# Three weights among the first loads, stage 0's parts of x between output copies, and attention units every nine products

## The chip, the cores and the metric

One core of one Trainium2 chip runs the whole kernel. The metric is the device time of one execution in microseconds (us), the median of several runs. The profile is of one further execution, taken by the hardware profiler. Engines: PE is TensorE, PEld its weight loads, DVE VectorE, ACT ScalarE, POOL GpSimd, and SP the engine that issues nearly all transfers; each runs its own instructions in program order, and engines wait for one another by semaphores. L522 is line 522 of the kernel.

## The reference

Masked attention for 8 batches of 8 heads (576 tokens, 64 values per head), and a feed-forward layer with the maximum of three products over its 4608 tokens of 512 values:

```python
mask_local = (rel >= 0) & (rel < 32)                    # heads 0 to 3
mask_strided = (rel >= 0) & (pos_q % 32 == pos_k % 32)  # heads 4 to 7
attn = softmax(where(mask, q @ k.T / 8, -1e9))
x = (attn @ v), heads side by side                      # 4608 x 512
h = max(x @ w1, x @ w2, x @ w3)                         # 4608 x 768
out = h @ w_out                                         # 4608 x 512
```

All values are float32. A product in full precision is made of three TensorE products of high and low parts (hi*hi, hi*lo, lo*hi).

## The kernel before, in words

**Attention units.** The attention comes in 32 units: unit n is batch n // 4 and one pair of heads, in the order strided, strided, local, local (`units`, L234). The heads of a pair lie in one quarter of x's 512 columns, so four units complete a batch's tokens. A unit runs through these steps, each named by a letter in the table `OPENING` (L58) and with its number behind it: S scores on TensorE into PSUM `s_ps` (L309, L318, L340); X mask and less the maximum on DVE (L361 to L368); E the exponential on ACT (L384, in one unit L376); N sums, division and transpose on DVE, from `s_ps` to `pt` (L394 to L404); V values on TensorE from `pt` and `v_t` into `o_ps` (L441, L470, L481); H a copy out of `o_ps` on ACT (L495), which is x's high part or x itself; L the low part on DVE (L500). Strided units of batch 1 and later also need U, `paired_queries` (L287): four ACT copies (L295) that lay out the queries in a `pt` tile, ahead of their scores. `pt` has two buffers, and so have queries and keys (`qk_t`) and values (`v_t`).

**Transfers.** SP issues loads and stores in program order, so whatever waits in its queue holds all behind it. First come the loads of the table `LOADS` (L54): `q` loads queries or keys of a unit (two issues), `v` a part of a unit's values (four or five issues), `w` the next of 18 pieces of w1, w2 and w3 (512 KB each). The pieces that `LOADS` leaves over, and six of w_out, follow at its end. Later a unit's loads are issued as an older unit's buffers come free.

**Weights.** Each piece is taken apart exactly into high and low parts: A and K on ACT (L164, L173), L165 on GpSimd, B on DVE (L183, L186), D on GpSimd (L196), C on ACT and GpSimd (L205, L206). A9 and K9, C8 stand for weight 9 and weight 8.

**Tokens 0 to 1023, plainly.** Two chunks of 512 tokens: `ff_in` (F; f and g are its halves, L522) makes one of 18 products x @ w per chunk into one of two PSUM banks, `ff_max` (M, L537 to L543) takes the maximum and splits h, `ff_out` (O, L552) multiplies by w_out, and `ff_store` (Q, L557) copies the result out of the bank on ACT into a `work` tile and has SP store it. Chunk 0 runs in the order of `OPENING`, chunk 1 in the loop at L720, with units 8 to 15 between its products. The half g0 needs x's parts of unit 3, so H3 and L3. T (L230, L231) splits chunk 1's x. `work` tiles are four, shared by the weights' parts, output copies and the sums below.

**Tokens 1024 to 4607, with fewer products.** The 3584 tokens go in four stages of two blocks of 448. Each stage computes two-by-two block products with seven products instead of eight (in the manner of Strassen and Winograd): nine groups (`quad`), each of seven products of six matmuls (L774), so 63 products per stage. The sums of weights that this needs are made by GpSimd during chunk 1 (L585, L593, L609, steps Y and Z and `sums_at`), written to DRAM (`scratch`), and streamed back as tiles `w_stream` (L665), nine tiles deep. The matching sums and parts of x are made by `conversion(s)` (L670): a generator of six parts of ACT casts (L677) and DVE differences (L680, L683), the fourth to sixth of which build on those before; stage 0's parts run among the four last output copies of chunk 1 (L745 to L747, and `list(convert)` for the rest), later stages' parts between a stage's output products. Each product's result is copied out of its bank by ACT (`snap`, L821, or L828), added by GpSimd (L833) and taken into the maximum `h_all` by DVE (L835). The product two behind uses the same bank. At a stage's end `split` (L858, L859) and `out_part` (L868) do h @ w_out, and `store` (L874) copies out.

**Units within the stages.** `before(s, k)` puts units 16 to 31 among the products k of a stage, six in stages 0 and 1 and four in stage 2 (`COUNTS`): `ahead` is S, the load of queries for two units later, and X; `placed` is V, the load of values, H and L. `after` gives E, N and U of the unit ahead two, three and four products later.

Of the kernel before, what the change touches and what calls it, by code (L numbers as in the profile page):

```python
# [40 lines left out]
COUNTS = (6, 6, 4, 0)  # L41
# [3 lines left out]
NJ = DF // P  # L45
# [6 lines left out]


LOADS = """  # L54
q0 q0 w0 w1 w2 w3 q1 q1 w4 q2 q2 v0 w5 v0 v0 v0 q3 q3 w6 v1 v1 v1 w7 w8 v1 v2 v2 v2 v2 v2 v3 v3 v3 v3 v3
q4 q4 v4 v4 v4 v4 w9 w10 w11 w12 w13 q5 q5 v5 v5 v5 v5
"""
OPENING = """  # L58
A0 S0 X0 A1 K0 E0 B0 B1 A2 K1 K2 D0 D1 C0 N0 S1 A3 K3 C1 B2 B3 A4 X1 D2 D3 B4 S2 E1 C2 N1 A5 K4 D4 C3 V0
# [3 lines left out]
B15 F8 W0 W1 W2 A17 X5 D15 M7 K16 C14 B16 F9 E5 C15 M8 K17 D16 B17 F10 W3 W4 N5 M9 M10 D17 F11 W5 A18 A19 B18 C16 K18 S6  # L63
B19 C17 A20 D18 K19 M11 A21 F12 W6 B20 K20 F13 W7 M12 X6 C18 H4 L4 D19 A22 K21 M13 F14 W8 D20 B21 C19 V5 M14 E6
H5 D21 A23 F15 B22 N6 K22 C20 F16 K23 C21 L5 M15 M16 D22 B23 S7 D23 C22 C23 F17 V6 M17 Y0 X7 O0 G7 Q0 T2 T3 O1 O2
N7 H6 U8 L6 Z0 V7 S8 Q1 Y1 T0 H7 X8 Q2 O3 E8 L7 T1 Q3 N8
"""
APART = [int(step[1:]) for step in OPENING.split() if step[0] == "G"]

# [2 lines left out]
def fused_kernel(ctx, tc, qT, kT, qk_loc, qk_str, v_loc, v_str, m_loc, m_str, w1, w2, w3, w_out, out):  # L72
# [214 lines left out]
    def paired_queries(n):  # L287

        t = loaded[n][0]
        qs = att.tile([P, 2, 512], F32, name="pt")  # L290
        to = qs.rearrange("p j (m r q) -> p j r m q", r=2, q=32)
        for x0, q0, w in ((0, 0, NI), (NI, NI, 32 - NI)):
            src = t[:, x0 : x0 + S].rearrange("p (j r m q) -> p j r m q", j=2, r=2, q=NI)
            for j in range(2):
                pin(nc.scalar.copy(out=to[:, j, :, :, q0 : q0 + w], in_=src[:, j, :, :, :w]))  # L295
        loaded[n].append(qs)
# [85 lines left out]
    def exponentials(n):  # L382
        s = state[n][1]
        pin(nc.scalar.activation(out=s, in_=s, func=AF.Exp, scale=SCALE))  # L384

    def probabilities(n):
        s_ps, s, wide, nm, at, axes, sm = state[n]
        if n in APART:
            sums = sm[:, :, :nm]
        else:  # L390
            sm = att.tile([P, 2, MS], F32, name="sm")

            sums = sm[:, :, :nm] if nm * at == 512 else s_ps[:, :, 512 - MS : 512 - MS + nm]
            pin(nc.vector.tensor_reduce(out=sums, in_=s, op=ALU.add, axis=axes))  # L394
        pin(nc.vector.tensor_scalar(out=sums, in0=sums, scalar1=EPS, scalar2=None, op0=ALU.add))
        pin(nc.vector.reciprocal(out=sm[:, :, :nm], in_=sums))
        pin(nc.vector.tensor_tensor(out=s, in0=s, in1=wide(sm), op=ALU.mult))
        state[n] = s_ps, nm, at

    def transposed(n):  # L400

        s_ps, nm, at = state[n]
        pt = att.tile([P, 2, 512], F32, name="pt")
        pin(nc.vector.transpose(pt[:, :, : nm * at], s_ps[:, :, : nm * at]))  # L404
        state[n] = pt
# [107 lines left out]
    def ff_in(c, j, i, heads=(2, 3, 0, 1)):  # L513

        if 2 in heads:
            hs[c, j, i] = bank()
        f_ps = hs[c, j, i]
        hi, lo = x_chunk(c)
        wh, wl = weight[i, j]
        for kc in heads:  # L520
            for n, (w, x) in enumerate(((wh, hi), (wh, lo), (wl, hi))):
                pin(nc.tensor.matmul(  # L522
                    f_ps, w[:, kc, :], x[:, kc, :], start=(kc == 2 and n == 0), stop=(kc == 1 and n == 2)
                ))
# [20 lines left out]
    def ff_out(c, t):  # L545
        f_ps = bank()
        ts = slice(t * P, (t + 1) * P)
        for j in range(NJ):
            hh, hl = hs[c, j]
            wh, wl = weight[None, j]  # L550
            for n, (h, w) in enumerate(((hh, wh), (hh, wl), (hl, wh))):
                pin(nc.tensor.matmul(f_ps, h[:, ts], w, start=(j == 0 and n == 0), stop=(j == NJ - 1 and n == 2)))  # L552
        hs[c, "out", t] = f_ps

    def ff_store(c, t):
        o_sb = wk.tile([P, DO], F32, name="work")
        pin(nc.scalar.copy(out=o_sb, in_=hs.pop((c, "out", t))))  # L557
        pin(nc.sync.dma_start(out=out[c * CH + t * P : c * CH + (t + 1) * P, :], in_=o_sb))
# [77 lines left out]
    for step in OPENING.split():  # L636
        what, n = step[0], int(step[1:])
# [8 lines left out]
    def ahead(n):  # L646

        scores(n)
        list(load_qk(n + 2))
        less_maximum(n)  # L650

    def placed(n):

        values(n)
        list(load_v(n + 2))
        leading(n)
        rest(n)
# [58 lines left out]
    sums_at = {-2: 1, 0: 2, 3: 3, 5: 4, 7: 5, 9: 6, 11: 7, 14: 8}  # L716
    coming, since = None, 0
    convert = iter(())
    paired_queries(9)
    for i in range(3 * NJ + CH // P):  # L720
        if i - 1 in first_bursts and first_bursts[i - 1] < 15:
            placed(first_bursts[i - 1])
        if i in first_bursts:
            if first_bursts[i] < 15:
                coming, since = first_bursts[i] + 1, i
                ahead(coming)
            else:
                placed(15)
        if i < 3 * NJ:
            ff_in(1, i // 3, i % 3)  # L730
        else:
            ff_out(1, i - 3 * NJ)
        if coming and i == since:
            exponentials(coming)
        if coming and i == since + 1:
            probabilities(coming)
            transposed(coming)
            if (coming + 1) % 4 in (0, 1):
                paired_queries(coming + 1)
            coming = None  # L740
        if i < 3 * NJ:
            ff_max(1, i // 3, i % 3)
        else:
            ff_store(1, i - 3 * NJ)
        if i >= 3 * NJ:  # L745
            for _ in range((2, 0, 1, 1)[i - 3 * NJ]):
                next(convert, None)  # L747
            load_next()
            load_next()
        if i - 3 in sums_at:  # L750
            build_high(sums_at[i - 3])
            build_low(sums_at[i - 3])
        if i in sums_at:
            build_sums(sums_at[i])
            build_mix(sums_at[i])
        if i == 3 * NJ - 1:
            late.close()
            plain.close()
            for name, bufs in (("xc", 1), ("wst", AHEAD + 1), ("snap", 8), ("hsp", 3)):
                second[name] = ctx.enter_context(tc.tile_pool(name=name, bufs=bufs, reuse_waits="tile"))  # L760
            convert = conversion(0)
# [6 lines left out]
    def supers():  # L768
# [9 lines left out]

        def before(s, k):

            n = 16 + sum(COUNTS[:s]) + k // 10
            if s == 0 and k == 1:
                ahead(16)
                running[:] = [16, k]
            elif k % 10 == 8 and k // 10 < COUNTS[s]:
                running[:] = []
                if n + 1 < len(units):
                    ahead(n + 1)
                    running[:] = [n + 1, k]
            elif k % 10 == 9 and k // 10 < COUNTS[s]:  # L790
                placed(n)

        def after(s, k):
# [11 lines left out]
        def quad(s, q):  # L805
# [6 lines left out]
            def go(out_, m, start=True):  # L812
                before(s, k[0])
                product(out_, m, x, stream.pop(0), start)
                load_next()
                after(s, k[0])
                k[0] += 1
# [61 lines left out]
        for s in range(NSUPER):  # L879
# [9 lines left out]
            convert = conversion(s + 1) if s + 1 < NSUPER else iter(())  # L889
# [77 lines left out]
```

## Time and profile before

| | |
|---|---|
| median of 3 runs | 684.23 us (682.28 to 685.16) |
| profiled execution | 683.3 us, of it the profile's span 681.6 us |
| TensorE busy | 649.3 us, 95% of the span |
| VectorE / ScalarE / GpSimd busy | 371.2 / 335.9 / 299.8 us |
| moved by DMA | 138.36 MB, 203 GB/s in the mean |

In rows of a timeline the first number is the start in us from the span's start, the second the length over all that the row joins; "x4" counts the instructions joined, and the brackets hold the idle time of the engine just before them and what ended it. A wait for several semaphores is put down to the one that came last by the profile. In rows of stages the first two numbers are from and to, the third the length; then come busy times by engine, the granted TensorE clock (1.00 is full), the share of the DMA engines' time, and GB/s. Rows of DMA issues end with KB each and the median us from issue to landing.

### The profile page before, as it was taken

The numbers are of one execution on the slowest core, as the hardware profiler recorded it, in microseconds if no ns is written. First come the engines' busy times: TensorE is split into PE (matmuls) and PEld (weight loads), VectorE is DVE, ScalarE is ACT, GpSimd is POOL, SyncE is SP. The second block draws the span as 40 slices with busy tenths as digits, with TensorE's granted clock in tenths as the row PEclk, the third lists the DMA queues.
The fourth block names the chain that finished last, engine by engine and source line by source line (L and its number), as shares of the span: only waits on it lengthen the run. The fifth ranks groups of instructions, "written<-read, shape, count | busy, mean of one in ns | idle before, by whom it ended". The sixth has DMA issues, their size and how long they took to land.

```text
span 681.6 us, 18034 instructions
## 1 busy us (share of the span) xinstructions
PE 649.3 (95%) x7408; PEld 554.2 (81%) x7408; DVE 371.2 (54%) x515; ACT 335.9 (49%) x702; POOL 299.8 (44%) x291
## 2 busy tenths in 40 slices
PE   3679999899998999999999999999999999999997
PEld 3458877778777888887888888789889988999986
DVE  5867965667657555468435556762651464124250
ACT  4767556334345444555455446554444554444431
POOL 8769898589950342430043342103244400444410
PEclk9779999999999999999999999999999999999999
DMA  9799873566689777773277778417767723777411
GB/s 299 204 288 367 287 251 121 183 187 203 197 260 324 235 237 241 255 228 121 86 248 247 242 235 246 144 70 191 236 201 201 217 70 107 215 216 217 136 46 63
DMA packets 89370, 138.36 MB, mean 203 GB/s; under 512 B 10152, under 2 KB 39592, under 8 KB 89288
## 3 DMA queue, kind: packets, MB, share of 16 engines
q1 hardware_dynamic: 85256, 129.86, 62.0%
q10 hardware_dynamic: 4032, 7.34, 2.9%
q8 instruction: 59, 0.97, 0.6%
q14 instruction: 23, 0.19, 0.1%
HBM read 111.21 MB, written 25.95 MB: 201 GB/s over the span
## 4 chain that ended last, share of the span: by engine, by line
PE 71%; POOL 9%; DMA 6%; issue 6%; DVE 4%; SPq 3%; ACT 2%; POOLq 0%; DVEq 0%; ACTq 0%
PE f_ps L774 40%; PE f_ps L868 15%; PE f_ps L522 8%; DMA w<-in_w 4%; PE f_ps L552 3%; POOL work L593 2%; PE o_ps L441 2%; POOL work L609 1%; POOL work L585 1%; PE s_ps L318 1%; POOL snap L833 1%; PE o_ps L470 1%; DVE h_all L835 1%; PE s_ps L340 1%; DMA out<-work 1%
## 5 line engine op out<-in xcount | busy, mean ns | idle before, releaser
L774 PE MATMUL f_ps<-xc,w_stream 128*128 128x448 f32 x1512 | 317.7, 368 | 1.8 <-ACT snap L821 1.8
L774 PEld LDWEIGHTS f_ps<-xc,w_stream 128*128 128x128 f32 x1512 | 280.8, 188 | 28.0 <-ACT snap L821 3.9
L821 ACT COPY snap<-f_ps 128x448 f32<-128x448 f32 x240 | 127.7, 533 | 159.2 <-PE f_ps L774 155.8
L833 POOL TENSOR_TENSOR snap<-snap 128x448 f32<-128x448 f32 x72 | 89.9, 1254 | 157.6 <-ACT snap L821 101.7
L835 DVE TENSOR_TENSOR h_all<-h_all,snap 128x448 f32<-128x448 f32 x96 | 77.7, 847 | 127.3 <-POOL snap L833 127.0
L868 PE MATMUL f_ps<-wNone,h_parts 128*128 128x512 f32 x504 | 115.6, 390 | 1.0 <-ACT h_parts L858 1.0
L833 POOL TENSOR_TENSOR h_all<-snap 128x448 f32<-128x448 f32 x36 | 41.3, 1149 | 164.5 <-ACT snap L821 162.9
L868 PEld LDWEIGHTS f_ps<-wNone,h_parts 128*128 128x128 f32 x504 | 94.3, 188 | 21.5 <-ACT h_parts L858 1.8
L522 PE MATMUL f_ps<-xh,w 128*128 128x512 f32 x288 | 97.4, 407 | 1.8 <-ACT xh L495 1.8
L522 PEld LDWEIGHTS f_ps<-xh,w 128*128 128x128 f32 x288 | 55.7, 194 | 14.9 <-ACT xh L495 2.3
L522 PE MATMUL f_ps<-xl,w 128*128 128x512 f32 x144 | 57.7, 401 | 0.1
L859 DVE TENSOR_TENSOR h_parts<-h_all,h_parts 128x768 fp32r<-128x768 f32 (+2 forms) x40 | 27.2, 712 | 25.9 <-ACT h_parts L858 25.7
L680 DVE TENSOR_TENSOR xc<-x_block,xc 128x896 fp32r<-128x896 f32 x28 | 29.9, 1087 | 18.1 <-ACT xc L677 18.1
L874 ACT COPY work<-f_ps 128x512 f32<-128x512 f32 x28 | 16.4, 586 | 41.7 <-PE f_ps L868 41.7
L858 ACT CAST h_parts<-h_all 128x768 fp32r<-128x768 f32 (+2 forms) x40 | 24.5, 642 | 17.7 <-DVE h_all L835 11.1
L404 DVE STREAM_TRANSPOSE pt<-s_ps 128x640 f32<-128x640 f32 (+2 forms) x32 | 32.5, 1016 | 1.1
L522 PEld LDWEIGHTS f_ps<-xl,w 128*128 128x128 f32 x144 | 27.9, 194 | 5.9 <-DVE xl L500 0.6
L552 PE MATMUL f_ps<-wNone,hh 128*128 128x512 f32 x96 | 30.9, 401 | 0.4 <-issue 0.4
L384 ACT ACTIVATE s_ps<-s_ps 128x640 f32<-128x640 f32 (+2 forms) x30 | 19.5, 651 | 23.3 <-DVE s_ps L368 23.3
L340 PEld LDWEIGHTS s_ps<-qk_t 64*32 64x32 f32 x1408 | 16.3, 114 | 17.1 <-DMA qk_t<-in_qT 8.2
L361 DVE TENSOR_TENSOR s_ps<-s_ps,mloc 128x640 f32<-128x640 f32 x14 | 11.6, 829 | 33.5 <-PE s_ps L340 33.5
L340 PE MATMUL s_ps<-qk_t 64*32 64x64 f32 (+1 forms) x1408 | 19.5, 227 | 10.1 <-DMA qk_t<-in_kT 7.6
(87 smaller groups left out, 701.1 us busy)
## 6 DMA issues: line engine op xcount, KB each, us to landing
w_stream<-scratch SPq DMA_DIRECT2D x252, 256.0 KB, 3.4
w<-in_w SPq DMA_DIRECT2D x18, 512.0 KB, 6.3
qk_t<-in_qT SPq DMA_DIRECT2D x28, 288.0 KB, 3.4
qk_t<-in_kT SPq DMA_DIRECT2D x28, 288.0 KB, 3.9
v_t<-in_v_str SPq DMA_DIRECT2D x56, 128.0 KB, 4.4
out<-work ACTq DMA_DIRECT2D x28, 256.0 KB, 2.1
scratch<-w SPq DMA_DIRECT2D x27, 256.0 KB, 3.5
v_t<-in_v_loc SPq DMA_DIRECT2D x48, 96.0 KB, 3.3
```

The lines of the kernel that those rows point to most:

```text
L340: pin(nc.tensor.matmul(s_ps[32 * j : 32 * (j + 1), h, k1 : k1 + w], t[hs, q0 : q0 + 32], t[hs, k0 : k0 + w], start=not first, stop=not fir ...
L404: pin(nc.vector.transpose(pt[:, :, : nm * at], s_ps[:, :, : nm * at]))
L522: pin(nc.tensor.matmul(f_ps, w[:, kc, :], x[:, kc, :], start=(kc == 2 and n == 0), stop=(kc == 1 and n == 2)))
L552: pin(nc.tensor.matmul(f_ps, h[:, ts], w, start=(j == 0 and n == 0), stop=(j == NJ - 1 and n == 2)))
L680: pin(nc.vector.tensor_tensor(out=x[m][:, 1], in0=src, in1=x[m][:, 0].bitcast(F32), op=ALU.subtract))
L774: pin(nc.tensor.matmul(out_, w[:, wl, fs], x[:, xl, k, :], start=start and k == 0 and n == 0, stop=k == 1 and n == 2, skip_group_check=not ...
L821: pin(nc.scalar.copy(out=t, in_=src))
L833: pin(nc.gpsimd.tensor_tensor(out=h if i == 0 else u, in0=u, in1=t, op=ALU.add))
L835: pin(nc.vector.tensor_tensor(out=h, in0=h, in1=u, op=ALU.max))
L858: pin(nc.scalar.copy(out=to[:, 0, j0:j1], in_=src))
L859: pin(nc.vector.tensor_tensor(out=to[:, 1, j0:j1], in0=src, in1=to[:, 0, j0:j1].bitcast(F32), op=ALU.subtract))
L868: pin(nc.tensor.matmul(outs[t], h, w, start=(j == 0 and n == 0), stop=(j == NJ - 1 and n == 2)))
```

## The change

There are four edits, and no instruction is added or taken away.

```diff
 LOADS = """
-q0 q0 w0 ... w7 w8 v1 v2 v2 v2 v2 v2 v3 v3 v3 v3 v3
-q4 q4 v4 v4 v4 v4 w9 w10 w11 w12 w13 q5 q5 v5 v5 v5 v5
+q0 q0 w0 ... w7 w8 v1 v2 w9 v2 v2 v2 w10 v2 q4 q4 v3 v3 w11 v3 v3 v3
+v4 v4 w12 v4 v4 w13 q5 q5 v5 v5 v5 v5
...
-N7 H6 U8 L6 Z0 V7 S8 Q1 Y1 T0 H7 X8 Q2 O3 E8 L7 T1 Q3 N8
+N7 H6 U8 L6 Z0 V7 S8 Q1 Y1 T0 H7 X8 Q2 O3 E8 L7 T1 U9 Q3 N8
...
-    paired_queries(9)
     for i in range(3 * NJ + CH // P):
...
         else:
+            before, behind = ((0, 2), (1, 1), (1, 1), (0, 0))[i - 3 * NJ]
+            for _ in range(before):
+                next(convert, None)
             ff_store(1, i - 3 * NJ)
+            for _ in range(behind):
+                next(convert, None)
         if i >= 3 * NJ:
-            for _ in range((2, 0, 1, 1)[i - 3 * NJ]):
-                next(convert, None)
             load_next()
             load_next()
...
-            n = 16 + sum(COUNTS[:s]) + k // 10
+            n = 16 + sum(COUNTS[:s]) + (k - 8) // 9
...
-            elif k % 10 == 8 and k // 10 < COUNTS[s]:
+            elif k % 9 == 8 and k // 9 < COUNTS[s]:
                 running[:] = []
                 if n + 1 < len(units):
                     ahead(n + 1)
...
-            elif k % 10 == 9 and k // 10 < COUNTS[s]:
+            elif k and k % 9 == 0 and k // 9 <= COUNTS[s]:
                 placed(n)
```

So: weights 9 to 11 are issued between the values of units 2 and 3, and weights 12 and 13 between those of unit 4; U9 comes ahead of Q3 in place of behind it; stage 0's six parts of x run two behind the first output copy, one ahead of and one behind each of the next two, where before they ran two behind the first, one behind each of the last two copies and the rest after; and in the stages a unit's scores come at products 8, 17, 26, 35, 44 and 53 (before: 8, 18, 28, 38, 48 and 58), its values one unit later, at 9, 18 and so on up to 54 (before 9, 19 up to 59). From L741 on the changed kernel's lines stand two or more further down (L774 becomes L776, L821 becomes L823).

SP's issues before, from the first parts of unit 2's values (the first L269 row) on; the tiles w_3 are weights 9 to 11:

```order
L269 DMA v_t<-in_v_loc 32x2x384 x3
L271 DMA v_t<-in_v_loc 32x2x192
L273 DMA v_t<-in_v_loc 32x2x64
L269 DMA v_t<-in_v_loc 32x2x384 x3
L271 DMA v_t<-in_v_loc 32x2x192
L273 DMA v_t<-in_v_loc 32x2x64
L246 DMA qk_t<-in_qT 128x576
L246 DMA qk_t<-in_kT 128x576
L280 DMA v_t<-in_v_str 32x2x512 x4
L152 DMA w_3_225<-in_w 128x4x256
L152 DMA w_3_227<-in_w 128x4x256
L152 DMA w_3_229<-in_w 128x4x256
```

And now, from behind the first part of unit 2's values to the last of unit 3's:

```order
L152 DMA w_3_207<-in_w 128x4x256
L269 DMA v_t<-in_v_loc 32x2x384 x2
L271 DMA v_t<-in_v_loc 32x2x192
L152 DMA w_3_212<-in_w 128x4x256
L273 DMA v_t<-in_v_loc 32x2x64
L246 DMA qk_t<-in_qT 128x576
L246 DMA qk_t<-in_kT 128x576
L269 DMA v_t<-in_v_loc 32x2x384 x2
L152 DMA w_3_221<-in_w 128x4x256
L269 DMA v_t<-in_v_loc 32x2x384
L271 DMA v_t<-in_v_loc 32x2x192
L273 DMA v_t<-in_v_loc 32x2x64
```

Three weights and unit 4's queries and keys now stand ahead of unit 3's last values, and two weights ahead of unit 2's.

ACT at the end of chunk 0, the difference of the two (L384 is E8, L230 is T1, L557 is Q3, L295 are U9's copies, L537 is chunk 1's first maximum):

```order
 L384 ACTIVATE s_ps<-s_ps 128x32x18
 L230 CAST xh<-x_one 128x512
+L295 COPY pt<-qk_t 128x2x8x18 x2
+L295 COPY pt<-qk_t 128x2x8x14 x2
 L557 COPY work<-f_ps_790 128x512
-L295 COPY pt<-qk_t 128x2x8x18 x2
-L295 COPY pt<-qk_t 128x2x8x14 x2
 L537 COPY h_max<-f_ps_791 128x512
```

U9's four copies moved ahead of the output copy; nothing else did there.

ACT at the end of chunk 1 before, from the second output copy to the first result of stage 0 (L557 are the output copies, L677 the casts of stage 0's parts of x, L821 the copy of a product's result):

```order
L557 COPY work<-f_ps_790 128x512
L557 COPY work<-f_ps_791 128x512
L677 CAST xc_2969<-x_block_1988 128x896
L677 CAST xc_2967<-x_block_1139 128x896
L557 COPY work<-f_ps_790 128x512
L677 CAST xc_2970<-x_block_1988 128x896
L677 CAST xc_2968<-x_block_1988 128x896
L677 CAST xc_2972<-x_block_1139 128x896
L821 COPY snap<-f_ps_791 128x448
```

And now the same stretch:

```order
L677 CAST xc_2969<-x_block_1988 128x896
L677 CAST xc_2967<-x_block_1139 128x896
L557 COPY work<-f_ps_790 128x512
L677 CAST xc_2970<-x_block_1988 128x896
L677 CAST xc_2968<-x_block_1988 128x896
L557 COPY work<-f_ps_791 128x512
L677 CAST xc_2972<-x_block_1139 128x896
L557 COPY work<-f_ps_790 128x512
L823 COPY snap<-f_ps_791 128x448
```

Two casts moved ahead of the second output copy, two ahead of the third and one ahead of the last, which is now directly followed by the first result of stage 0.

More of the change, by code (lines that the diff above doesn't have):

```diff
@@ L54 @@
 LOADS = """
-q0 q0 w0 w1 w2 w3 q1 q1 w4 q2 q2 v0 w5 v0 v0 v0 q3 q3 w6 v1 v1 v1 w7 w8 v1 v2 v2 v2 v2 v2 v3 v3 v3 v3 v3
-q4 q4 v4 v4 v4 v4 w9 w10 w11 w12 w13 q5 q5 v5 v5 v5 v5
+q0 q0 w0 w1 w2 w3 q1 q1 w4 q2 q2 v0 w5 v0 v0 v0 q3 q3 w6 v1 v1 v1 w7 w8 v1 v2 w9 v2 v2 v2 w10 v2 q4 q4 v3 v3 w11 v3 v3 v3
+v4 v4 w12 v4 v4 w13 q5 q5 v5 v5 v5 v5
 """
```

## The prediction

> **What bounds the kernel now.** I read the page first: the busy shares and the chain that ended last.
>
> ```profile
> PE 649.3 (95%) x7408; PEld 554.2 (81%) x7408; DVE 371.2 (54%) x515; ACT 335.9 (49%) x702; POOL 299.8 (44%) x291
> PE 71%; POOL 9%; DMA 6%; issue 6%; DVE 4%; SPq 3%; ACT 2%; POOLq 0%; DVEq 0%; ACTq 0%
> ```
>
> TensorE is busy for 649.3 of 681.6 us and carries 71% of the chain. The change removes no matmul, so it can only win some of the 32.3 us in which TensorE stands still, and what counts is which of those holes the edits touch. Next I asked for the busy time by stage over the early holes. Behind the colon stand the length, each engine's busy time, the granted TensorE clock, the DMA share and GB/s.
>
> ```profile
> 28.00:34.00 6.00, 3.16 (x177) 2.86 (x177) 4.69 (x10) 5.04 (x12) 4.30 (x4) 0.50 0.45 101
> 40.00:44.00 4.00, 2.01 (x87) 1.35 (x75) 2.22 (x3) 0.58 (x2) 1.71 (x2) 1.00 0.90 298
> 44.00:46.50 2.50, 0.76 (x1) 0.29 (x1) 0.67 (x2) 2.50 (x8) 1.89 (x3) 0.50 1.06 345
> 46.50:50.50 4.00, 3.90 (x10) 3.09 (x10) 2.85 (x5) 3.30 (x7) 3.21 (x6) 0.50 1.04 275
> 50.50:58.00 7.50, 7.50 (x33) 6.14 (x33) 6.99 (x12) 5.65 (x13) 7.50 (x7) 0.98 1.10 315
> ```
>
> Two things are to be seen. From 28 to 34 us the DMA engines moved 101 GB/s, while a full queue moves 275 to 345. And from 40 to 46.5 us TensorE worked 2.77 of 6.5 us, after which ten matmuls ran at half clock (0.40 us each, against 7.5/33 = 0.23). Then I followed each hole in the timelines. There are four that the edits reach.
>
> **Part one: three weights sent earlier.** The timelines of ACT, then of TensorE, then of SP's issues (start, length, what, idle time before it and who ended it):
>
> ```profile
> 38.92 0.62 ACT L205 CAST w<-work 128x512 fp32r<-128x512 f32 x1 [1.56 <-POOL work L196]
> 43.42 0.66 ACT L164 ACTIVATE work<-w 128x512 f32<-128x512 f32 x1 [3.88 <-DMA w<-in_w]
> 45.05 0.64 ACT L495 CAST xh<-o_ps 128x480 fp32r<-128x480 f32 x2
> ...
> 39.80 0.47 PE L441 MATMUL o_ps<-pt,v_t 32*64 32x64 f32 x26
> 42.16 0.85 PE L441 MATMUL o_ps<-pt,v_t 32*64 32x64 f32 x58 [1.89 <-issue]
> 45.74 0.80 PE L522 MATMUL f_ps<-xh,w 128*128 128x512 f32 x1 [1.83 <-ACT xh L495]
> 46.64 0.80 PE L522 MATMUL f_ps<-xl,w 128*128 128x512 f32 x1
> ...
> 24.43 1.93 SPq L269 DMA_DIRECT2D v_t<-in_v_loc  x3
> 36.05 6.04 SPq L152 DMA_DIRECT2D w<-in_w  x5
> ```
>
> ACT stood 3.88 us for weight 9 (step A9), which SP issued only at 36.05. Behind A9, in program order, wait K9, C8 and H3 (L495), and H3 is what the matmul at 45.74 waited for. Unit 3's values (V3, L441) had been done since 43.01, so H3 came 2.0 us late because of a weight that nobody needed yet. In the new order weight 9 follows the first of the three issues at 24.43, so it goes out at about 25.1 us. A9 then starts as C7 ends (39.5), H3 could start 45.05 - 43.42 = 1.63 us later (41.2), and so V3's end releases it: H3 at 43.1. That is 1.95 us earlier, for TensorE, and equally for the conversions behind H3 on ACT and with them for GpSimd. The 1.89 us inside V3, where TensorE waited for nothing that the profile shows, I leave as they are.
>
> The price is that values and queries now stand behind weights in SP's queue. Rows for it: the page's DMA issues, and V2 on TensorE.
>
> ```profile
> w<-in_w SPq DMA_DIRECT2D x18, 512.0 KB, 6.3
> qk_t<-in_qT SPq DMA_DIRECT2D x28, 288.0 KB, 3.4
> ...
> 32.37 1.26 PE L441 MATMUL o_ps<-pt,v_t 32*64 32x64 f32 x59 [1.53 <-DVE xl L500]
> ```
>
> Ahead of unit 2's last part there now lie two weights more, 1.05 MB, which the half-empty stretch from 28 us on carries in 3.5 us at 298 GB/s: 31.5 us, plus what was left of unit 2's own parts. V2 starts at 32.37, so it comes between 0 and 0.6 us late; I take 0.25. Ahead of unit 3's last part lie three weights and one unit's q and k more, 2.16 MB, with the 0.6 MB that moved there anyway 2.8 MB, done at 28 + 2.8/0.298 = 37.3 us. V3 starts at 39.80, so 2.5 us of cover are left; without them V3 would be late by as much as is missing. Of SP's own work nothing is added, only its order. **Term: 1.95 - 0.25 = 1.7 us**, bounds 0 (V3 two us late) and 5.7 (a rival below).
>
> One thing could add to it: the half clock. If it ends 3.9 us after the flow restarts, as before (46.64 to 50.5), the ten slow matmuls only move along, and the term stays. [...]
>
> **Part two: U9 ahead of Q3.** ACT, TensorE, DVE, and GpSimd at that place:
>
> ```profile
> 124.95 0.58 ACT L557 COPY work<-f_ps 128x512 f32<-128x512 f32 x1 [4.43 <-DMA out<-work]
> 125.44 1.33 ACT L295 COPY pt<-qk_t 128x288 f32<-128x288 f32 x4
> ...
> 126.54 1.41 PE L318 MATMUL s_ps<-qk_t,pt 64*64 64x36 f32 x64 [1.90 <-ACT pt L295]
> ...
> 123.74 1.25 DVE L404 STREAM_TRANSPOSE pt<-s_ps 128x1024 f32<-128x1024 f32 x1
> ...
> 136.35 1.29 POOL L543 TENSOR_TENSOR hl<-h_max,hh 128x512 fp32r<-128x512 f32 x1 [0.60 <-ACT hh L542]
> 138.83 1.29 POOL L609 TENSOR_TENSOR work<-work,sums_high 128x512 fp32r<-128x512 f32 x1 [1.19 <-ACT sums_high L603]
> ```
>
> ACT waited 4.43 us with Q3 (L557) for an output store to free a buffer, and the four query copies of U9 (L295) stood behind it; unit 9's scores on TensorE waited 1.90 us for them. Ahead of Q3, U9 runs inside that wait and is done at about 121.9. What is late next is DVE: the transpose of unit 8 (L404) reads the score bank until 124.99, and unit 9's scores overwrite it. So they start at 125.0, not 126.54: 1.5 us. The product behind them needs the bank that Q3 frees at 125.53, while the scores, at the 1.41 us that they took, run until 126.4; that is cover enough. GpSimd must follow: its long stretch of sums begins at 138.83, after idle pieces of 0.60 and 1.19 us that both end with ACT work released by TensorE, so up to 1.79 us of it can follow. U9 costs nothing new: its ACT time of 1.33 lies in the wait. **Term: 1.5 us**, bounds 0 and 1.8.
>
> **Part three: stage 0's parts of x.** ACT, DVE, TensorE, SP, and the landing of the stream's loads issued from 207 us:
>
> ```profile
> 206.50 0.59 ACT L557 COPY work<-f_ps 128x512 f32<-128x512 f32 x1 [3.66 <-PE f_ps L552]
> 206.99 1.78 ACT L677 CAST xc<-x_block 128x896 fp32r<-128x896 f32 x2
> 215.41 0.96 ACT L821 COPY snap<-f_ps 128x448 f32<-128x448 f32 x2
> ...
> 207.97 1.09 DVE L680 TENSOR_TENSOR xc<-x_block,xc 128x896 fp32r<-128x896 f32 x1 [7.06 <-ACT xc L677]
> ...
> 215.99 3.91 PE L774 MATMUL f_ps<-xc,w_stream 128*128 128x448 f32 x18 [1.67 <-ACT snap L821]
> 220.07 3.92 PE L774 MATMUL f_ps<-xc,w_stream 128*128 128x448 f32 x18 [0.17 <-ACT snap L821]
> ...
> 207.48 1.01 SPq L665 DMA_DIRECT2D w_stream<-scratch  x2
> ...
> w_stream<-scratch SPq DMA_DIRECT2D x2, 256.0 KB, 5.0
> ```
>
> DVE idled 7.06 us because ACT's next conversion stood behind two output copies. It then finished the parts so late that ACT's first snap (L821) ran at 215.41, and TensorE stood 1.67 us, and 0.17 us later on. In the new order the third part runs on ACT before the second output copy, and only one cast is left behind the third, so everything is converted before the last output copy. ACT has room for it: it stood 3.66 us ahead of one of these copies. What is late next are the stream's loads: the product that now starts at 214.3 needs the pair issued at 207.48, landed at 212.5 to 213.5. That just fits; each us that they are late is a us of this term. **Term: 1.8 us**, bounds 0 and 1.84.
>
> **Part four: units every nine products.** No work is added; the same instructions of a unit come one product earlier per unit, five by a stage's end. The two holes at stage ends, and DVE ahead of the first:
>
> ```profile
> 312.82 17.34 PE L868 MATMUL f_ps<-wNone,h_parts 128*128 128x512 f32 x75 [0.40 <-ACT h_parts L858]
> 434.69 23.48 PE L868 MATMUL f_ps<-wNone,h_parts 128*128 128x512 f32 x102 [0.59 <-ACT h_parts L858]
> ...
> 308.25 0.82 DVE L394 TENSOR_REDUCE s_ps<-s_ps 128x10 f32<-128x640 f32 x1
> 311.21 1.12 DVE L835 TENSOR_TENSOR h_all<-h_all,snap 128x448 f32<-128x448 f32 x2
> ```
>
> DVE's last maxima came at 311.21 because the next unit's softmax, from 308.25, was queued ahead of them; that softmax now starts at product 53 of 63 and is done. **Term: 0.40 + 0.59 = 1.0 us**, bounds 1.0 and a loss (last rival).
>
> **The sum.** 1.7 + 1.5 + 1.8 + 1.0 = 6.0 us. The profiled execution took 683.3 us (span 681.6 and 1.7 around it): 677.3. It lies 0.9 below the median of 684.23, from which the same sum gives 678.2. I forecast 677.5.
>
> **The rivals.** The first: GpSimd holds the second half.
>
> ```profile
> 139.00:195.00 56.00, 55.33 (x971) 44.02 (x970) 39.78 (x58) 22.39 (x53) 54.12 (x54) 1.00 0.67 205
> ...
> ACT snap L821 <- PE f_ps L774: 155.8, 213, 2.4
> ```
>
> In these 56 us GpSimd is busy for 54.12 and TensorE for 55.33: both are near their bound. If GpSimd's stretch did not start earlier, what TensorE won before 139 us would be spent in new waits by 195 us, and parts three and four alone remain: 683.3 - 2.8 = 680.5. Against it stand the 1.79 us of idle pieces just ahead of the stretch, and that ACT and GpSimd gain in part one as much as TensorE.
>
> The second: unit 3's values come late and the first hole stays, 683.3 - 4.3 = 679.0. [...] By rows it decides if those 2.8 MB need until 41.8 us, 203 GB/s; no full stretch above moved less than 275.
>
> The third: the first hole closes wholly. If the 1.89 us inside V3 go too, V3 ends at 41.1, the fall of the clock at 44.0 does not come, and the first ten matmuls after the restart end at 42.8 + 10 x 0.23 = 45.1 rather than 50.6: 5.5 to 5.7 in place of 1.7, 673.4. For it speaks only that this wait ended by no engine; against it that the queue stays full there.
>
> The fourth is slower: with a unit every nine products its scores, exponential and copies fall on other products of the seven-product round than before (on the sixth, for one), and ACT's snaps come late once per unit. Place: L821 and the product two behind it. Sixteen units pay it, so from 6.0/16 = 0.38 us per unit on it eats the gain and from 0.59 the kernel is slower than any run shown; one wait like the 1.67 at 215.99 in each would make it 677.3 + 26.7 = 704. Against it: ACT itself waited for TensorE at 213 of 240 snaps, 155.8 us in all.
>
> **How the numbers follow.** Forecast 0.62, GpSimd 0.13, values late 0.12, hole wholly closed 0.09, snaps late 0.04. A measurement here can tell about 0.5%, 3.4 us, from no change: faster is below 680.8, slower above 687.6. Faster takes 0.60 of the forecast, 0.06 of the first rival, which lies on the line, 0.08 of the second and all of the third: 0.83. Slower is the fourth, 0.04; the rest is 0.13. The range runs from the third rival (673.5) to the first with part four at nothing (681.5) and half a us of the runs' own spread: 682.0.
>
> **What would show it.** Right: weight 9's cast on ACT (L164 behind the cast at about 39) without a DMA wait, H3 some 2 us earlier, no wait for pt ahead of unit 9's scores, no hole ahead of the third product, none over 0.1 at the ends of stages 0 and 1, and TensorE's busy time unchanged. Wrong: V2 or V3 waiting for v_t, a new wait of TensorE between 139 and 195 us, or TensorE waiting for snaps inside the stages; and wrong in any case if TensorE's busy time itself grows.

## The result, and the profile after

| | before | after |
|---|---|---|
| median of the runs taken together | 684.69 us (682.28 to 688.07, 4 runs) | 675.52 us (675.31 to 676.76, 4 runs) |
| profiled execution, of it the span | 683.3, 681.6 us | 676.8, 675.1 us |
| TensorE busy | 649.3 us | 649.4 us |

The ratio is 0.9866, with a 95% interval of 0.9822 to 0.991: faster, by less than 2%. (The ratios here and below are not the quotients of the two medians.) Measured again, the same kernel took 676.65 us (675.32 to 678.07, 6 runs), a ratio of 0.9898 [0.9874, 0.9923]. The first two traces differ by 6.5 us, the medians by 9.2 and 6.4; the second trace of the changed kernel is 8.0 us ahead of that of before. Every experiment below stands beside runs of the kernel before that were made with it; their medians lie between 683.05 and 684.38 us.

The page of after, its busy shares, its chain, and the group of stage products:

```profile
PE 649.4 (96%) x7408; PEld 554.7 (82%) x7408; DVE 375.0 (56%) x515; ACT 336.6 (50%) x702; POOL 299.7 (44%) x291
PE 89%; DMA 5%; SPq 2%; DVE 2%; ACT 1%; issue 1%; ACTq 0%; DVEq 0%
L776 PE MATMUL f_ps<-xc,w_stream 128*128 128x448 f32 x1512 | 318.1, 368 | 0.8 <-issue 0.6
L870 PE MATMUL f_ps<-wNone,h_parts 128*128 128x512 f32 x504 | 115.0, 389 | 0.0
```

TensorE's work is the same to 0.1 us and its idle time fell from 32.3 to 25.7. GpSimd has left the chain (9% before), "issue" went from 6% to 1%, and the 1512 matmuls of the stage products wait 0.8 us in all. The stages of the first hole, now:

```profile
28.00:34.00 6.00, 2.58 (x152) 2.35 (x156) 4.54 (x8) 5.21 (x17) 3.09 (x3) 1.00 0.99 263
40.00:44.00 4.00, 4.00 (x155) 3.26 (x153) 2.66 (x6) 2.28 (x4) 3.69 (x4) 1.00 1.01 213
44.00:46.50 2.50, 1.68 (x8) 0.99 (x7) 2.36 (x5) 2.16 (x6) 2.50 (x4) 1.00 1.14 261
46.50:50.50 4.00, 4.00 (x19) 3.31 (x18) 3.79 (x7) 3.16 (x6) 3.48 (x4) 1.00 1.03 233
```

From 28 to 34 us the transfers run at 263 GB/s where they ran at 101, and from 40 to 46.5 us TensorE works 5.68 us where it worked 2.77. From 28 to 34 us it works less than before (2.58, was 3.16). Part of that is the price, the 0.70 us below; part is that V1 started 1.25 us later in this execution (30.20, was 28.95). The timeline of after, for parts one, two, three and four in this order:

```profile
33.62 0.72 PE L441 MATMUL o_ps<-pt,v_t 32*64 32x64 f32 x28 [1.52 <-DVE xl L500]
35.04 0.74 PE L441 MATMUL o_ps<-pt,v_t 32*64 32x32 f32 x31 [0.70 <-DMA v_t<-in_v_loc]
42.88 1.14 PE L441 MATMUL o_ps<-pt,v_t 32*64 32x64 f32 x84
41.56 0.67 ACT L164 ACTIVATE work<-w 128x512 f32<-128x512 f32 x1
44.07 0.65 ACT L495 CAST xh<-o_ps 128x480 fp32r<-128x480 f32 x2 [0.76 <-PE o_ps L441]
...
119.08 1.34 ACT L295 COPY pt<-qk_t 128x288 f32<-128x288 f32 x4
124.39 0.59 ACT L557 COPY work<-f_ps 128x512 f32<-128x512 f32 x1 [3.96 <-DMA out<-work]
122.43 1.25 DVE L404 STREAM_TRANSPOSE pt<-s_ps 128x1024 f32<-128x1024 f32 x1
123.78 1.14 PE L318 MATMUL s_ps<-qk_t,pt 64*64 64x36 f32 x64
136.01 2.54 POOL L609 TENSOR_TENSOR work<-work,sums_high 128x512 fp32r<-128x512 f32 x2
...
205.68 1.09 DVE L680 TENSOR_TENSOR xc<-x_block,xc 128x896 fp32r<-128x896 f32 x1 [0.36 <-ACT xc L677]
210.28 8.98 PE L776 MATMUL f_ps<-xc,w_stream 128*128 128x448 f32 x42
...
298.81 0.85 DVE L404 STREAM_TRANSPOSE pt<-s_ps 128x640 f32<-128x640 f32 x1
302.36 28.75 PE L870 MATMUL f_ps<-wNone,h_parts 128*128 128x512 f32 x126
```

Part one: weight 9's cast (41.56) waits for no transfer any more, and H3 (44.07) follows V3's end (44.02) at once; but V2 now stands 0.70 us for values that come behind two weights. Part two: U9's copies run at 119.08 inside ACT's wait for the store, unit 9's scores start as the transpose that frees their bank ends (122.43 + 1.25), and GpSimd's long stretch starts at 136.01 (138.83 before). Part three: the last part of x is done at 206.8, ahead of the first product (207.90), and the 42 matmuls from 210.28 on, seven products, stand in one row without a hole. Part four: the unit's softmax ends at 299.7, before the last maxima start (300.75), and the output products are one row of 126 matmuls without a hole.

### The profile page after: what moved, and what is told of

It is laid out like the page before. It is cut to its first block, busy times and chain, and to the rows that moved or that the text cites. A ratio compares the mean times of both kernels' runs of the same rounds, so it can differ in the third digit from the quotient of the medians.

```text
span 675.1 us, 18032 instructions
## 1 busy us (share of the span) xinstructions
PE 649.4 (96%) x7408; PEld 554.7 (82%) x7408; DVE 375.0 (56%) x515; ACT 336.6 (50%) x702; POOL 299.7 (44%) x291
## 4 chain that ended last, share of the span: by engine, by line
PE 89%; DMA 5%; SPq 2%; DVE 2%; ACT 1%; issue 1%; ACTq 0%; DVEq 0%
PE f_ps L776 46%; PE f_ps L870 17%; PE f_ps L522 14%; PE f_ps L552 4%; DMA w<-in_w 3%; PE o_ps L441 3%; PE o_ps L470 2%; PE s_ps L318 2%; PE s_ps L340 2%; DMA v_t<-in_v_loc 1%; DMA out<-work 1%; SPq L280 1%; SPq L152 1%; SPq L246 0%; SPq L269 0%
## 5 line engine op out<-in xcount | busy, mean ns | idle before, releaser
L776 PE MATMUL f_ps<-xc,w_stream 128*128 128x448 f32 x1512 | 318.1, 368 | 0.8 <-issue 0.6
L776 PEld LDWEIGHTS f_ps<-xc,w_stream 128*128 128x128 f32 x1512 | 280.4, 188 | 27.7 <-ACT snap L823 2.5
L823 ACT COPY snap<-f_ps 128x448 f32<-128x448 f32 x240 | 128.0, 533 | 165.9 <-PE f_ps L776 163.9
L837 DVE TENSOR_TENSOR h_all<-h_all,snap 128x448 f32<-128x448 f32 x96 | 80.2, 876 | 130.0 <-POOL snap L835 129.9
L384 ACT ACTIVATE s_ps<-s_ps 128x640 f32<-128x640 f32 (+2 forms) x30 | 19.5, 651 | 20.4 <-DVE s_ps L368 20.4
L677 ACT CAST xc<-x_block 128x896 fp32r<-128x896 f32 x28 | 25.7, 943 | 3.3 <-DVE xc L680 1.2
```

The lines of the kernel that those rows point to most:

```text
L677: pin(nc.scalar.copy(out=x[m][:, 0], in_=src))
L776: pin(nc.tensor.matmul(out_, w[:, wl, fs], x[:, xl, k, :], start=start and k == 0 and n == 0, stop=k == 1 and n == 2, skip_group_check=not ...
L823: pin(nc.scalar.copy(out=t, in_=src))
L837: pin(nc.vector.tensor_tensor(out=h, in0=h, in1=u, op=ALU.max))
```

## The experiments

Each part was first made alone, on the kernel before. Time between landmarks in the traces, in us, each the difference of the starts (or first start and last end) of TensorE's rows:

| | before | after | after, measured again | part alone |
|---|---|---|---|---|
| unit 7's scores start at | 96.92 | 95.59 | 95.42 | 95.54 (one) |
| unit 7's values to unit 9's scores | 11.90 | 10.48 | 10.42 | 10.43 (two) |
| first product to unit 17's scores | 13.46 | 11.30 | 11.22 | 11.24 (three) |
| output products of stage 0 | 29.47 | 28.75 | 28.72 | 28.75 (four) |
| output products of stage 1 | 29.72 | 28.74 | 28.74 | 28.74 (four) |

The first row needs care: with part two alone, and so with the old loads, unit 7's scores start at 95.38. More on this below.

**Part one alone**: the kernel before with the first hunk of the change only (the two lines of `LOADS`).

> The kernel before with the new order of loads alone. My account (each edit closes its own hole, and the engines behind follow): H3 no longer waits behind weight 9, unit 7's values start about 113.3 (114.64 before), and the 1.3 us are still there at unit 15's values, so the time is 1.3 to 1.7 us below before, ratio 0.998. Rival, GpSimd holds: the lead is spent by unit 15's values, ratio 1.000. Rival, the start carries the difference between 6.5 us in the two traces and 9.2 us in the medians: this edit alone gives 4 us or more, ratio 0.994 or less.

Measured: 682.61 us (680.64 to 688.44, 12 runs) beside 683.33, ratio 1.0016 [0.9993, 1.004]: no gain. TensorE, ACT and GpSimd:

```profile
33.84 0.75 PE L441 MATMUL o_ps<-pt,v_t 32*64 32x64 f32 x28 [1.53 <-DVE xl L500]
35.78 1.24 PE L441 MATMUL o_ps<-pt,v_t 32*64 32x32 f32 x56 [1.19 <-DMA v_t<-in_v_loc]
44.11 0.65 ACT L495 CAST xh<-o_ps 128x480 fp32r<-128x480 f32 x2 [0.58 <-PE o_ps L441]
125.25 1.49 PE L318 MATMUL s_ps<-qk_t,pt 64*64 64x36 f32 x64 [1.78 <-ACT pt L295]
127.69 1.05 PE L522 MATMUL f_ps<-xh,w 128*128 128x512 f32 x2
139.13 2.54 POOL L609 TENSOR_TENSOR work<-work,sums_high 128x512 fp32r<-128x512 f32 x2 [1.04 <-ACT sums_high L603]
```

The mechanism is there (H3 right behind V3, V2 1.19 us late), and unit 7's scores come 1.4 us earlier. But the hole ahead of unit 9's scores remains (1.78), in this execution the granted clock fell to 0.50 from 127 to 129 us behind it (1.05 us for two matmuls), and GpSimd's stretch starts at 139.13, no earlier than before: in this trace the lead is gone by 139 us.

**Part two alone**: the second and third hunks (`L7 T1 U9 Q3 N8` in `OPENING`, and no `paired_queries(9)` ahead of chunk 1).

> The kernel before with U9 ahead of Q3 alone. My account: from the start of unit 7's values to that of unit 9's scores 10.5 us in place of 11.9, GpSimd's stretch of sums starts as much earlier, and unit 15's values too: 1.4 us less, ratio 0.998. Rival, GpSimd holds: unit 15's values start where they did (196.3) with a longer wait ahead, ratio 1.000.

Measured: 680.42 us (678.02 to 685.26, 12 runs), ratio 0.9965 [0.9941, 0.999]. GpSimd and TensorE:

```profile
123.58 1.14 PE L318 MATMUL s_ps<-qk_t,pt 64*64 64x36 f32 x64 [0.71 <-issue]
135.99 2.55 POOL L609 TENSOR_TENSOR work<-work,sums_high 128x512 fp32r<-128x512 f32 x2
```

GpSimd's stretch follows, from 138.83 to 135.99, and unit 15's values come as much earlier (193.46, were 196.30): the rival that GpSimd holds the second half is false. Of these 2.84 us only half is the work of part two. The other half was there at unit 7's values already (113.15, were 114.64), with the old loads: the start differs from execution to execution.

**Part three alone**: `ff_store` between its `before` and `behind` conversions.

> The kernel before with stage 0's parts of x spread over the output copies alone. My account: no hole ahead of the third product of stage 0 (1.67 us before) and none at the sixth (0.17), from the first product to unit 17's scores 11.3 us in place of 13.5: 1.8 to 2.1 us less, ratio 0.997. Rival, the stream's loads are late: a hole of 0.5 us or more for w_stream stays in the first eight products, and less than 1.3 us is won.

Measured: 681.63 us (679.55 to 685.23), ratio 0.9988 [0.9966, 1.0011], 1.7 us by medians. TensorE has no hole, and the stretch of 42 matmuls takes 8.93 us in one row:

```profile
212.18 8.93 PE L777 MATMUL f_ps<-xc,w_stream 128*128 128x448 f32 x42
```

**Part four alone**: `k % 9` and `(k - 8) // 9` in `before(s, k)`.

> The kernel before with units every nine products alone. My account: only the holes at the ends of stages 0 and 1 go; the two output parts, 29.5 and 29.7 us before, take 28.75 each: 1.7 us less, ratio 0.9975, and the products of a stage take the same time as before (92.2 us in stage 1). Rival, snaps late: 6 us or more slower. Rival, the spacing itself gains inside the stages: 3 us or more less, with stage 1's products below 91.5 us.

Measured: 682.75 us (680.82 to 689.1), ratio 1.0007 [0.9982, 1.0032], 0.6 us by medians. The trace shows the two stage ends whole, 1.70 us in sum:

```profile
306.10 28.75 PE L868 MATMUL f_ps<-wNone,h_parts 128*128 128x512 f32 x126
427.04 28.74 PE L868 MATMUL f_ps<-wNone,h_parts 128*128 128x512 f32 x126
```

Parts one, three and four are each too small to be told from no change. The four differences by medians (0.7, 2.9, 1.7, 0.6) sum to 5.9, beside a forecast of 6.0. By the ratios the same runs give only 1.6 us in sum (1.1 slower, 2.4 and 0.8 faster, 0.5 slower), each with some 1.6 us either way. So these times do not confirm the sum of the parts; what the parts do is read from the landmarks above.

**Closer still**: the changed kernel with a unit every eight products.

```diff
-            n = 16 + sum(COUNTS[:s]) + (k - 8) // 9
+            n = 16 + sum(COUNTS[:s]) + (k - 8) // 8
-            elif k % 9 == 8 and k // 9 < COUNTS[s]:
+            elif k and k % 8 == 0 and k // 8 <= COUNTS[s]:
-            elif k and k % 9 == 0 and k // 9 <= COUNTS[s]:
+            elif k > 1 and k % 8 == 1 and k // 8 <= COUNTS[s]:
```

> The changed kernel with units every eight products (scores at products 8, 16, 24 and on, values one unit later at 9, 17 and on). My account: the holes at the stage ends are closed already, so the same time as the changed kernel within 1 us, about 675.5. Rival, the spacing itself gains: 1.5 us or more less. Rival, snaps late: TensorE waits for snaps in the stages, 2 us or more slower than the changed kernel.

Measured: 680.87 us (677.05 to 687.45, 12 runs), ratio 0.9964 [0.9932, 0.9996]. The output products are no better (28.75 and 28.74), and TensorE now waits for DVE inside the stages; DVE in this trace, the same DVE instruction in the trace of after, and TensorE in three places:

```profile
54.35 6.48 DVE L395 TENSOR_SCALAR sm<-sm 128x16 f32<-128x16 f32 x1
55.95 0.35 DVE L395 TENSOR_SCALAR sm<-sm 128x16 f32<-128x16 f32 x1
63.30 1.94 PE L318 MATMUL s_ps<-qk_t,pt 64*64 64x36 f32 x64 [5.91 <-issue]
...
251.18 0.97 PE L340 MATMUL s_ps<-qk_t 64*32 64x64 f32 x72 [0.84 <-DVE pt L404]
372.95 1.14 PE L318 MATMUL s_ps<-qk_t,pt 64*64 64x36 f32 x64 [0.78 <-DVE pt L404]
```

A unit's scores then come while the transpose of the unit ahead still reads the bank; eight is too close. From the first product to the last output matmul this trace takes 466.2 us, those of the changed kernel 463.5 and 462.8. The 5.91 us stand in no other trace: one small DVE instruction (54.35) took 6.48 us where it took 0.35 in after (55.95), and the scores waited for the transpose behind it. Why it was slow is not known.

**The price of part one taken away**: the changed kernel, with weight 9 behind all of unit 2's values, weights 10 and 11 behind unit 3's.

```diff
-... w7 w8 v1 v2 w9 v2 v2 v2 w10 v2 q4 q4 v3 v3 w11 v3 v3 v3
-v4 v4 w12 v4 v4 w13 q5 q5 v5 v5 v5 v5
+... w7 w8 v1 v2 v2 v2 v2 v2 w9 v3 v3 v3 v3 v3 q4 q4 w10 w11
+v4 v4 w12 v4 v4 w13 q5 q5 v5 v5 v5 v5
```

> The changed kernel with weights 9 to 11 sent a little later: weight 9 behind all of unit 2's values, weights 10 and 11 behind unit 3's values and unit 4's queries and keys. My account: V2 no longer waits for v_t (0.70 us in the changed kernel) and V2, f0 and f1 end 1 to 2 us earlier, weight 9 is still in time for A9; 0.5 to 1.5 us less than the changed kernel at unit 7's values. Rival: V2's delay in the changed kernel's trace is of that execution and not of the order, then nothing is won.

> The changed kernel once more, for a second trace and more times beside the two above. My account: about 675.5, ratio to before 0.987 to 0.990. If the 6.5 us between the first two traces are the truth and the 9.2 between the medians chance, the ratio is 0.990; if the kernel before varies at its start and its trace was one of its better runs, it is 0.987.

Measured: 678.06 us (676.98 to 680.61, 6 runs), ratio 0.992 [0.9892, 0.9949], beside 676.65 and 0.9898 for the changed kernel as it is. V2 waits for no values, and nothing is won. The delay of V2 does belong to the new order, though: four traces with it show 0.45 to 1.19 us, none with the old. This trace:

```profile
31.91 1.90 PE L481 MATMUL o_ps<-pt,v_t 18*64 18x18 f32 x116 [3.11 <-DMA v_t<-in_v_str]
35.33 1.88 PE L441 MATMUL o_ps<-pt,v_t 32*64 32x64 f32 x84 [1.53 <-DVE xl L500]
45.23 0.85 PE L441 MATMUL o_ps<-pt,v_t 32*64 32x64 f32 x58 [1.99 <-issue]
```

In this trace V1 came late (3.11) and V3 had a hole of 1.99 us ended by "issue", as before had one of 1.89.

**Part one in company**: the changed kernel with the old `LOADS`, and before with the first three hunks (parts one and two).

> The changed kernel with the old table of loads: parts two, three and four without part one. Theory: part one is worth about 1.0 us, the difference of the mean starts of unit 7's scores (96.55 with the old loads in four traces, 95.5 with the new in three), and this stays when unit 9's copies are moved too. Then the ratio to before is 0.990 to 0.994 (parts two to four alone gave -2.9, -1.7 and -0.6 us by medians, -5.2 in sum), the median about 1 us above the changed kernel's own, and unit 7's scores start at 96 to 97 us. Rival: part one is worth nothing also here, as it was by itself (ratio 1.0016); then the ratio is that of the changed kernel, 0.987 to 0.990. Forecast theory (1.7 us): 0.992 to 0.995.

> Before with the new loads and unit 9's copies moved, without parts three and four. Theory: with U9 out of the way GpSimd follows both, and the lead of part one is kept: long stretch of GpSimd's sums (its first sum by L609 there) at 135 us or earlier (135.99 with U9 alone, 139.13 with the loads alone), unit 15's values at 192.5 to 193.3 (193.46 with U9 alone), ratio 0.993 to 0.996. Rival: the lead ends somewhere else before 139 us even so, because GpSimd or a store holds it: unit 15's values at 193.4 or later and the ratio that of U9 alone, 0.9965.

Measured: without part one 677.78 us (676.05 to 679.37, 6 runs), ratio 0.9929 [0.9906, 0.9953]; parts one and two 679.68 us (678.08 to 683.28, 12 runs), ratio 0.9945 [0.9926, 0.9964], part two alone 0.9965. Part one is worth 2 us by the one pair (0.9929 against 0.9898; 1.1 by the medians, which were not measured together), 1.4 by the other (0.9965 against 0.9945), and nothing alone; the intervals of each pair overlap. That it is worth something in company is not settled: the span of the trace without part one is 674.8 us, those of the changed kernel are 675.1 and 673.6. The trace of parts one and two, from the slowest of its twelve runs (683.28 us), did not show the expected lead: unit 15's values start at 196.39, against 193.46 with part two alone. TensorE lost 4.9 us in two holes there:

```profile
32.53 1.26 PE L481 MATMUL o_ps<-pt,v_t 18*64 18x18 f32 x69 [2.28 <-issue]
35.31 1.26 PE L441 MATMUL o_ps<-pt,v_t 32*64 32x64 f32 x59 [1.53 <-DVE xl L500]
39.19 0.67 PE L441 MATMUL o_ps<-pt,v_t 32*64 32x64 f32 x25 [2.62 <-issue]
```

**What "issue" is.** These two holes lie 69 + 59 = 128 recorded matmuls apart. The queues' rows of before and, in stretches of 0.1 us, the one packet of the instruction queue ahead of the hole at 42.16 in before:

```profile
q8 instruction: 59, 0.97, 0.6%
q8 instruction: 1, 0.02, 154.6%
```

A packet holds 0.97 MB / 59 = 16 KB, and 59 of them go with 2 x 7408 = 14,816 recorded matmuls and weight loads: 251 per packet, if all are TensorE's, or about 126 matmuls with their weight loads. That is an estimate, and close to the 128 between the holes. The packet of the second row starts between 38.2 and 38.3 us and takes 1.546 x 0.1 x 16 = 2.5 us (0.9 to 1.8 elsewhere); V3's hole ends 1.4 us behind its end. In the eleven traces up to here every hole of TensorE of 0.25 us or more that "issue" ended in the first 121 us, the 5.91 us above apart, ends 2.4 to 3.0 us behind the start of such a packet (3.7 and 3.9 where the packet itself was slow) and 1.3 to 1.6 us behind its end. So the theory is that TensorE waits for its own instructions. To test it, small matmuls were put into the 7.5 us in which TensorE waits for unit 1's keys, in the changed kernel; their result is overwritten:

```diff
         first = b == 0
+        for _ in range(32 if n == 1 else 0):
+            pin(nc.tensor.matmul(s_ps[:32, 0, :NI], loaded[0][0][:D, :32], loaded[0][0][:D, S : S + NI], start=True, stop=True))
         if first:
```

> The changed kernel with 32 small float32 matmuls more (64 recorded matmuls with 64 weight loads, 128 instructions, half of what one 16 KB packet of the instruction queue q8 holds) ahead of unit 1's masks, where TensorE waits 7.5 us for unit 1's keys anyway; their result is overwritten. What it asks: whether the holes that the profile ends by issue are TensorE waiting for its own instructions. Theory: in every trace these holes end 2.4 to 3.0 us behind the start of a 16 KB instruction packet (3.7 to 4.0 where the packet itself took 2.2 to 2.5 us), about 1.5 us behind its end; moved by half a packet the boundaries fall elsewhere, so the hole of 0.57 to 0.89 us inside unit 5's values at 65 us (five traces of seven with units every nine products or new loads) and the one of 0.18 to 0.85 us ahead of chunk 0's output products at 118 us are gone or stand 64 recorded matmuls earlier or later, and every hole still ends 2.4 to 3.0 us behind a packet's start. Rival: TensorE stands there for a reason of those places (a bank, a queue of its own); then the holes stay where they were. Time: within 3 us of the changed kernel either way, 674 to 679 us.

The second kernel has 64 in place of 32.

> The same with 64 small float32 matmuls (256 instructions, one whole packet). Theory: the boundaries fall at the same places of the program as in the changed kernel, one packet later in number, so the holes inside unit 5's values and ahead of chunk 0's output products are back, 0.3 to 0.9 us. Rival: no difference between this run and the one with half a packet. Time: within 2 us of the changed kernel, 675 to 678 us.

Measured: 683.93 us (682.53 to 685.79, 12 runs), ratio 0.9991 [0.9965, 1.0016], and 680.72 us (679.12 to 684.6, 12 runs), ratio 0.9942 [0.9916, 0.9968]. Against the changed kernel (676.65, 0.9898) half a packet costs 6.4 us by the ratios and 7.3 by the medians, a whole one 3.0 and 4.1: far outside what was expected for the half, and beyond it for the whole. TensorE with 32:

```profile
5.80 3.52 PE L307 MATMUL s_ps<-qk_t 64*32 64x18 f32 x63
14.74 1.74 PE L342 MATMUL s_ps<-qk_t 64*32 64x18 f32 x128 [4.15 <-DMA qk_t<-in_kT]
21.42 1.01 PE L342 MATMUL s_ps<-qk_t 64*32 64x64 f32 x55 [2.46 <-issue]
26.08 1.06 PE L483 MATMUL o_ps<-pt,v_t 18*64 18x18 f32 x56 [2.44 <-issue]
37.33 0.41 PE L483 MATMUL o_ps<-pt,v_t 18*64 18x18 f32 x5 [2.35 <-issue]
52.56 0.79 PE L524 MATMUL f_ps<-xh,w 128*128 128x512 f32 x1 [1.55 <-issue]
```

The added work was over at 9.3 us, and unit 1's scores start at 14.74 as in after (14.80): nothing on the path until then. Then TensorE runs dry five times (those four and 1.84 at 32.68), each time until 2.6 to 3.0 us behind a packet's start, and unit 6's scores come at 85.49 instead of 79.10. Behind them the landmarks of TensorE lie 5.4 to 6.4 us later than in after, with no further loss. The two holes of the changed kernel that the expectation named (in the values at 65 us, which are unit 4's, and ahead of chunk 0's output products) are gone. What settles it is the count of TensorE's recorded matmuls ahead of each hole: 348, 476, 731 and 858 in before, 348, 476, 603 and 731 in parts one and two, and 349, 476, 604 and 731 here, though the 64 added ones are among them. So the holes stand at fixed numbers of instructions, some 128 matmuls or a multiple of that apart, and not at places of the program: that half of the theory holds and the rival, a reason of those places, is false. With 64 more the holes stand behind 222, 350, 476, 604, 731 and 859, and the queue moved one packet more:

```profile
q8 instruction: 60, 0.98, 0.6%
```

The other half failed: a whole packet does not restore the old pattern (only the hole ahead of the output products is back, 0.65), and the first hole (1.25) falls among the added matmuls; why was not shown. Small matmuls were thus not free here even where TensorE was idle: 32 of them, 64 as recorded, cost 6.4 us and 64 of them 3.0, by the ratios.

## Why the prediction was right, point by point

**The sum.** By traces the parts gave 1.34 (unit 7's values at 113.30 for 114.64), 1.42, 2.16 and 1.70 us, 6.6 in sum, for 6.5 measured and 6.0 forecast. 677.5 was forecast; the medians were 675.52 and 676.65. That the sum fits so well is partly luck: most of the 1.34 is not the work of part one, as the next paragraphs show, and parts three and four gave 1.1 us more than their terms.

**Part one: mechanism right, size wrong, and not settled to a microsecond.** The step "H3 could start 1.63 us later, and so V3's end releases it ... 1.95 us earlier" was read from one execution. From V3's end to H3 the five traces with the old loads take 2.04 (before), 1.41, 1.37, 1.73 and 1.15 us, those with the new 0.03 to 0.1: the gain is 1.5 in the mean. The step "between 0 and 0.6 us late; I take 0.25" is the one that failed. V2 stood 0.70, 0.90 and 1.19 us for its values in after, its second trace and part one alone, and 0.45 with units every eight products: 0.8 in the mean. (In parts one and two, where TensorE was late already, it did not wait.) The working counted bytes, which gave 31.5 us. In after V2's last part was issued at 30.08 us (27.04 before), and V2 could go on with it at 35.04. So 1.5 - 0.8 = 0.7 us is left of 1.7, and V2 waiting for v_t, which the prediction names as a sign of being wrong, was seen. V3 came in time in all of these, so the rival that unit 3's values come late is false. The rows from which both are read, in old order (without part one), then in new (the second trace of after):

```profile
41.97 1.15 PE L441 MATMUL o_ps<-pt,v_t 32*64 32x64 f32 x84
42.64 0.67 ACT L164 ACTIVATE work<-w 128x512 f32<-128x512 f32 x1 [1.85 <-DMA w<-in_w]
44.27 0.64 ACT L495 CAST xh<-o_ps 128x480 fp32r<-128x480 f32 x2
```

```profile
36.18 1.18 PE L441 MATMUL o_ps<-pt,v_t 32*64 32x32 f32 x56 [0.90 <-DMA v_t<-in_v_loc]
42.80 1.15 PE L441 MATMUL o_ps<-pt,v_t 32*64 32x64 f32 x84
43.98 0.65 ACT L495 CAST xh<-o_ps 128x480 fp32r<-128x480 f32 x2
```

How much of it reaches TensorE is read best from V2's first matmul, which stands ahead of all that the new order touches, to unit 7's scores. With the old loads this takes 64.55 us in before, but 61.72 to 61.79 in the four other traces; with the new it takes 61.97, 60.86 and 61.70 in after, its second trace and part one alone. Beside those four, part one is worth 0.2 us in the mean. Its lead is there at unit 5's scores, which start 25.39, 24.38 and 25.17 us behind V2 (25.41 to 26.39 in the four with the old loads). It goes behind them: from unit 4's values to unit 6's scores the three take 16.0 to 16.1 us (14.9 to 15.8 in the four), and 0.78 to 0.89 us of that is a hole in unit 4's values ended by "issue", which of the four only the changed kernel with the old loads has (0.57). What the trace of before has more is above all the hole of 1.89 inside V3, which the prediction left as it is. The runs point to a wait for instructions there, which comes in some executions of either order (1.99 in V3 with weight 9 moved back).

The step that the ten slow matmuls behind the restart "only move along" failed too. With the new loads there are none there in the same three traces. With the old, before and parts two, three and four alone have 9 or 10 of them (0.43 us each), but the changed kernel with the old loads has none, so the loads alone do not decide it. The third rival's two events, no hole in V3 and no slow matmuls behind the restart, did come in the trace of after, but not its 5.5 us: V1 and V2 came later there, and 11 matmuls were slow ahead of V3, where before had 6.

The record of the granted clock does not show every slow stretch: before's stands at 0.50 from 44.0 us to the end of the ten slow matmuls, but after's stays at 1.00 from the start of the span to its end, though three matmuls took 1.28 us in it (from 37.72 to 39.00, 0.43 each, against 0.23 later).

**Part two: right.** 1.42 us against 1.5; the transpose of unit 8 was next late, as forecast, and GpSimd followed, by more than the 1.79 us of its idle pieces (2.82), since what stands ahead of them moved too. By medians it is the largest part, 2.9 us alone, twice what its landmarks show (11.90 to 10.43).

**Part three: right, a little more.** 2.16 against 1.8: the two holes (1.84) and 0.3 us beside them. The stream's loads, named as next late, were not late.

**Part four: right, undersized.** "0.40 + 0.59 = 1.0 us" took the idle time in the rows; the output products as a whole shrank by 0.72 and 0.98, 1.7 us. The row of the hole gave 0.40 for stage 0, the whole stretch 0.72: what a hole costs is read better from the length of the stretch around it. The fourth rival (snaps late with nine) is false: the snaps wait 163.9 us for TensorE, more than the 155.8 before, and stage 1's products take 92.25 us (92.17).

## What to carry to other kernels

A load that nobody needs yet can still hold the path, through the program order of the engine that converts it (ACT stood 3.88 us for weight 9 in before); moving it ahead can cost what stands behind it in the same queue (V2 stood 0.45 to 1.19 us for its values in four traces), and both are to be read from several executions, since the gain differed here by 0.9 us from one to the next and the price by 0.7. Where the start of a kernel varies, measure a part between two landmarks close around it, not from the start: part one seemed to be worth 1.34 us in one pair of traces, and 0.2 between landmarks in seven. Put work without a new input ahead of a copy that waits (parts two and three, 1.42 and 2.16 us by the traces), and look for the engine that is next late. And count instructions, not only busy time: where many small matmuls stand close together, TensorE ran dry of them here for up to 2.67 us at a time.

## What the runs showed of the hardware that was not expected

The instruction queue moves packets of 16 KB (59 of them, 0.97 MB), by the estimate above some 250 of TensorE's instructions each, and in the first 70 us, where 128 small matmuls with their weight loads take 1.5 to 2.1 us (128 in 1.45, 116 in 1.90), TensorE ran dry for up to 2.67 us at a time; the profile calls this "issue". How often this comes differs: there is none between 27 and 47.5 us in the traces of parts two and three alone, and 7.1 us in all between 20 and 40 us in that of parts one and two. What makes a packet come late is not known. Instructions added there were not free: 32 small float32 matmuls more cost 6.4 us by the ratios and 7.3 by the medians. The start of this kernel differs accordingly: in the eleven traces without added matmuls, whose kernels are alike up to there in everything but the loads, unit 6's scores start between 78.89 and 82.00 us, and at 84.98 behind the slow DVE instruction above. How much of that is waits for instructions was not measured one by one.
